# Scores of three head pairs in fp32 on the two row halves, without scales and splits, and a new order of all instructions

## The chip, the core and the metric

The kernel runs on one core of a Trainium2 chip. The engines are PE (TensorE: matrix products), DVE (VectorE), ACT (ScalarE), POOL (GpSimd) and SP (SyncE, which here only issues DMAs). The metric is the device time of one execution in microseconds, lower being better; the time of a kernel is the median of several runs.

## The reference, cut to what matters

Four batches of eight heads with 1152 keys and values of 64 elements. Queries are averaged in twos, so there are 576 of them. Attention is followed by a two-layer network with an ELU between the layers.

```python
q_pool = q.reshape(B, H, S // 2, 2, D).mean(axis=3)      # 4, 8, 576, 64
scores = np.matmul(q_pool, k.transpose(0, 1, 3, 2)) / np.sqrt(D)
scores = scores - np.max(scores, axis=-1, keepdims=True)
attn = np.exp(scores)
attn = attn / (np.sum(attn, axis=-1, keepdims=True) + 1e-09)
out = np.matmul(attn, v)                                 # 4, 8, 576, 64
x = out.transpose(0, 2, 1, 3).reshape(2304, 512)
h = x @ w_in                                             # 2304, 2048
g = np.where(h > 0, h, np.exp(np.minimum(h, 0)) - 1)
return g @ w_out                                         # 2304, 512
```

All inputs and the output are fp32.

## The kernel before

**Tiles.** The four batches are the kernel's units 0 to 3. In each, two heads go together as a pair, so a unit has four pairs. A pair has nine steps of attention: four steps of 128 pooled queries for either head, and one in which the last 64 queries of both heads share the 128 rows. That makes 36 steps in a unit and 144 in all.

**A step.** `scores` (L903, L908, L917) puts 128 x 1152 scores into the tile `s`, of which there is one. `biggest` (L932, DVE) copies the scores, scaled and with their sign turned, to a tile `ep` and takes the extreme of each row on the way. `expo` (L938, ACT) makes the exponentials and their sum. A reciprocal follows (`recip` on DVE, L946 and L947, or on POOL, L498 and L955). From there a pair goes one of two ways, by a letter in the table `SPLIT`. In a pair with "f", the probabilities are normalised in fp32 (L958 POOL, L961 DVE or L964 ACT), turned by 128 x 128 blocks on PE (L1015), copied out by ACT (L1025) or DVE (L1028) and multiplied by v in fp32 (L1047). In a pair with "s" they are split into two f16 halves (L983 POOL or L986 ACT for the high half, L989 on DVE for the low one), turned by DMA, and multiplied by split values (L1059).

**How a score is made exact in f16.** `prep` makes q and k ready for a pair. The sums of absolute values of q and k (`absum`, L558, ACT) give a power of two for each through a product with ones on PE (`summed`, L535) and four small DVE operations (L650, L492, L493, L498). With these scales q and k are split into a high f16 half (`hi`, L564 on ACT or L498 on POOL) and a low one (`lo`, L578 on DVE or L498 and L584 on POOL). In pairs 1 to 15 DMAs then turn q and k (L660, L711) and copy q's halves (L705, L708). In pair 0 (`dup`) PE turns them instead: `turned` issues 36 f16 products with a halved identity (L681), and ACT copies the results out (L684). A score is then six products: three of high with high and low together (512, 512 and 128 columns, L903), one of 128 columns (L908), and two of 512 columns that use only 64 rows of the array each and lie side by side on its two row halves (L917).

**Weights.** Both layers' weights arrive in 64-bit words. DVE decodes each piece of 512 words with three instructions (L789, L790, L793), 32 pieces in all. They are scaled and split like q and k (L816, L819, and L825 on POOL). All of that falls into unit 0. The first layer's products are L1158 and the second's L1240. Both wait for a batch's attention, so unit 0's attention has none of them to run beside it until its end.

**What sets the order.** The table `ORDER` lists every task by number with a letter for its engine: p is PE, v DVE, a ACT, g POOL, s the DMA queue of SP. The program is emitted in just that order, and each engine works through its own list strictly in turn. The table `SLOTS` names the buffer of each tile. A score task whose shape of PE's array would differ from that of the task before it issues L917 first (`turned`).

Of the kernel before, what the change touches and what calls it, by code (L numbers as in the profile page):

```python
# [32 lines left out]
0s 3s 1v 317s 2a 5a 6p 10g 337s 312s 393s 311s 7v 319v 21a 8a 22v 31p 23p 9v 11p 12a 32a 29p 25p  # L33
339v 36s 30a 27p 17p 314v 28a 395v 24a 306s 322s 438p 19p 33s 439v 13p 26a 14a 440a 441g 18a 313v
451p 38a 321s 332s 452v 308v 442a 453a 454g 15p 462p 34v 35a 39p 20a 336s 455a 463v 464a 16a 465g
324v 40v 41a 427p 447p 456p 460p 445p 46g 342s 428v 42v 4s 466a 486p 446a 43s 461a 471p 334v 429a
315a 49s 487v 458p 488a 469p 523p 457v 430g 431g 467p 472a 459v 489g 524v 468a 470a 448a 432p 436p
434p 44s 307s 437a 433v 525a 490a 475p 476v 477a 435a 47g 48s 526v 527v 510p 511v 443p 532p 338v
530p 533a 528p 531a 529a 512a 45s 50g 499p 473p 444a 449p 500v 547p 323v 51a 344v 340a 548v 513g
514a 491p 501a 52s 309v 478v 316s 325a 450a 474a 584p 492a 585v 502g 54a 479g 327s 392s 549a 503a  # L40
55p 519p 495p 496a 534p 586a 318v 536p 493p 494a 482p 483a 56v 517p 587g 537v 57a 508p 58v 509v
571p 572v 588a 518a 506p 331s 538a 62g 63g 535v 341s 539v 550v 37s 65s 310a 520a 573a 507a 504p
505v 326s 560p 561v 589p 480p 595p 484p 593p 591p 64s 540g 481a 333v 551a 59s 320a 592a 343v 485a
497p 68s 543p 590a 594a 345a 596v 328v 335a 498a 552p 553a 545p 515p 516a 556p 608p 394v 546a 562a
# [12 lines left out]
715p 790v 91v 747a 722p 767a 749a 402s 768g 726p 727v 692v 723v 378s 367s 776p 756g 777v 725a 95a
# [176 lines left out]
"""  # L234
SPLIT = ("ffff", "ssss", "ssfs", "ssss")


class Port(float):
# [99 lines left out]
def attention_moe_kernel(  # L338
# [208 lines left out]
    def prep(pr, t0, t1):  # L547
# [116 lines left out]
        def turned(name, what, key, after, bufs, to):  # L664
# [21 lines left out]
            def first_out_dve():  # L686
                nc.vector.tensor_copy(dst(), src())
# [626 lines left out]
```

## Time and profile before

| | us |
|---|---|
| median of 3 runs | 761.78 (761.12 to 762.26) |
| the profiled execution's own time | 760.01 |
| its span | 758.2 |
| PE busy | 708.5 (93%) |
| DVE busy | 628.1 (83%) |
| ACT busy | 593.5 (78%) |
| POOL busy | 372.2 (49%) |

The span is the profiled execution from its first to its last instruction; the 1.8 us around it belong to that execution's time. The profile was taken once, the median is of other runs. A busy share is an average over stages that differ: unit 0 with its weights first, then three units of attention beside the products of the batch before, and last the products of unit 3.

### The profile page before, as it was taken

The page shows a single profiled execution, that of the slowest core. Times are in us where ns is not written, and L with a number is a line of the kernel's source. Part 1 is how long each engine was busy: PE and PEld are TensorE (multiplying, and loading weights), DVE is VectorE, ACT ScalarE, POOL GpSimd, SP SyncE. Part 2 cuts the span into 40 slices and gives each one's busy share as a digit, 9 for nine tenths or more (in the row PEclk, how much of TensorE's full clock was granted, in tenths as well). Part 3 has the DMA queues.
Part 4 walks back from the last instruction along what each step waited for, and adds up shares of the span by engine and source line. Part 5 has one row for each costly group of instructions (what it writes and reads, how often), then busy time and mean ns, then how long its engine had stood idle before and what let it go on. Part 6 is the DMA issues. An engine that isn't in the chain of part 4 may idle for free. (4 is left out here: it accounts for less than half of the span.)

```text
span 758.2 us, 19529 instructions
## 1 busy us (share of the span) xinstructions
PE 708.5 (93%) x7795; PEld 468.7 (62%) x7795; DVE 628.1 (83%) x1108; ACT 593.5 (78%) x997; POOL 372.2 (49%) x396
## 2 busy tenths in 40 slices
PE   2678899999999999999999999899999999999997
PEld 1356576777555755775566566677566655775753
DVE  5999999999999988878888888989988978775331
ACT  4899899999999967797598768899888755773542
POOL 0253856659435556586424653567636345421231
PEclk9999999999999999999999999999999999999999
DMA  8688774629799999999999997899999999764001
GB/s 270 205 264 209 167 257 143 182 67 186 161 194 201 193 190 199 161 193 188 208 203 214 179 214 145 157 195 205 180 187 191 170 189 165 122 113 95 24 1 35
DMA packets 315818, 129.38 MB, mean 171 GB/s; under 512 B 290064, under 2 KB 292112, under 8 KB 315728
## 3 DMA queue, kind: packets, MB, share of 16 engines
q1 hardware_dynamic: 315728, 128.15, 84.4%
q8 instruction: 61, 1.00, 0.6%
q14 instruction: 29, 0.24, 0.1%
HBM read 45.09 MB, written 4.72 MB: 66 GB/s over the span
## 5 line engine op out<-in xcount | busy, mean ns | idle before, releaser
L932 DVE TENSOR_SCALAR_CACHE_REDUCE ep<-s,sm 128x1152 f32<-128x1152 f32 x138 | 194.8, 1412 | 23.9 <-PE s L917 12.0
L938 ACT ACTIVATE ep<-ep,wk 128x1152 f32<-128x1152 f32 x138 | 173.0, 1254 | 41.0 <-DVE ep L932 38.0
L1158 PE MATMUL r<-x,wi 128*128 128x256 f16 (+1 forms) x1536 | 197.4, 286 | 1.4 <-DVE x L1136 1.4
L1240 PE MATMUL r<-wo,g 128*128 128x512 f16 (+1 forms) x864 | 175.3, 379 | 0.6 <-POOL g L1212 0.6
L1158 PEld LDWEIGHTS <-wi 128*128 128x128 f16 x1536 | 147.8, 98 | 45.0 <-issue 6.9
L989 DVE SCALAR_TENSOR_TENSOR ep<-ep,wk,hb 128x1152 f16<-128x1152 f32 x99 | 145.7, 1479 | 12.1 <-POOL hb L983 7.1
L1240 PEld LDWEIGHTS <-g 128*128 128x128 f16 (+1 forms) x864 | 74.2, 100 | 83.3 <-issue 3.8
L903 PE MATMUL s<-kT,qT 128*128 128x512 f16 (+3 forms) x480 | 96.7, 333 | 16.8 <-DVE ep L932 11.8
L986 ACT ACTIVATE hb<-ep,wk 128x1152 f16<-128x1152 f32 x59 | 73.7, 1249 | 23.3 <-POOL wk L955 13.3
L1059 PEld LDWEIGHTS <-v 128*64 128x64 f16 x2970 | 77.9, 110 | 11.8 <-issue 11.0
L1059 PE MATMUL r<-pT,v 128*64 128x128 f16 (+1 forms) x2970 | 84.4, 215 | 0.7 <-DMA pT<-ep 0.7
L498 POOL TENSOR_SCALAR wk<-wk 128x1 f32<-128x1 f32 x61 | 23.9, 391 | 121.5 <-ACT ep L938 117.9
L903 PEld LDWEIGHTS <-qT 128*128 128x128 f16 (+1 forms) x480 | 39.2, 101 | 59.6 <-issue 34.1
L1212 POOL TENSOR_TENSOR g<-tmp,g 128x320 f16<-128x320 f32 (+1 forms) x57 | 59.0, 1040 | 33.9 <-ACT g L1208 32.7
L983 POOL TENSOR_SCALAR hb<-ep,wk 128x1152 f16<-128x1152 f32 x40 | 57.9, 1448 | 34.1 <-DMA pT<-hb 10.1
L1194 DVE SCALAR_TENSOR_TENSOR tmp<-r,tmp 128x320 f32<-128x320 f32 (+1 forms) x96 | 52.2, 550 | 21.9 <-POOL tmp L1179 12.9
L1171 ACT ACTIVATE tmp<-r 128x320 f32<-128x320 f32 (+1 forms) x96 | 45.4, 476 | 23.4 <-PE r L1158 22.3
L917 PE MATMUL s<-kT,qT 64*128 64x512 f16 (+1 forms) x320 | 57.4, 394 | 3.5 <-DVE ep L932 2.9
L1174 ACT ACTIVATE tmp<-tmp,us 128x320 f32<-128x320 f32 (+1 forms) x96 | 58.1, 611 | 1.8
L1015 PE MATMUL r<-ident,ep 128*128 128x128 f32 x351 | 50.8, 284 | 4.4 <-DVE tmp L1194 1.2
L1179 POOL TENSOR_SCALAR tmp<-tmp,us 128x320 f32<-128x320 f32 (+1 forms) x32 | 24.3, 761 | 56.7 <-ACT tmp L1174 56.3
L1216 POOL TENSOR_SCALAR g<-tmp 128x320 f16<-128x320 f32 (+1 forms) x41 | 27.1, 662 | 47.2 <-DVE tmp L1194 40.7
(149 smaller groups left out, 1047.1 us busy)
## 6 DMA issues: line engine op xcount, KB each, us to landing
k<-in_k_dram SPq DMA_DIRECT2D x16, 576.0 KB, 4.6
v<-in_v_dram SPq DMA_DIRECT2D x16, 576.0 KB, 5.0
q<-in_q_dram SPq DMA_DIRECT2D x16, 512.0 KB, 4.6
g<-in_moe_w_out_dram SPq DMA_DIRECT2D x16, 512.0 KB, 4.6
g<-in_moe_w_in_dram SPq DMA_DIRECT2D x13, 512.0 KB, 5.6
qT<-qT SPq DMA_DIRECT2D x45, 144.0 KB, 2.8
out_dram<-tmp SPq DMA_DIRECT2D x16, 256.0 KB, 3.1
pT<-ep SPq DMA_TRANSPOSE x99, 3.7
```

Source lines behind the costliest of these rows:

```text
L903: nc.tensor.matmul(s.ap[rows, c, 0:n], pr.qT.ap[:, 0, j, rows], keys[h][c], start=first[c], stop=not first[c] and c < 2, skip_group_check= ...
L917: nc.tensor.matmul(s.ap[rows, c, 0:512], pr.qT.ap[r, 1, j, rows], keys[h][c][r], start=first[c], stop=not first[c], skip_group_check=True,)
L932: nc.vector.tensor_scalar(e_(), s.ap.rearrange("p a b -> p (a b)")[:, 0:S], pr.sm.ap[:, 12:13], None, op0=ALU.mult, op1=ALU.min, accum_out ...
L938: nc.scalar.activation(out=e_(), in_=e_(), func=AF.Exp, bias=nm.ap[:, 0:1], scale=-1.0, accum_out=nm.ap[:, 1:2],)
L983: nc.gpsimd.tensor_scalar(hb.ap, e_(), nm.ap[:, 1:2], 1.0, op0=ALU.mult, op1=ALU.mult)
L986: nc.scalar.activation(out=hb.ap, in_=e_(), func=AF.Copy, scale=nm.ap[:, 1:2])
L989: nc.vector.scalar_tensor_tensor(out=e16(), in0=e_(), scalar=nm.ap[:, 1:2], in1=hb.ap, op0=ALU.mult, op1=ALU.subtract)
L1059: nc.tensor.matmul(half(h), pr.v16.ap[:, h, order[c], e], p, start=(j + c == 0), stop=(j == 2 and c == NCH - 1), skip_group_check=True,)
L1158: nc.tensor.matmul(hp.ap[:, f * n:(f + 1) * n], w_in16[g][:, a, c, (f0 + f) * 128:(f0 + f + 1) * 128], x16.ap[:, e, c, g0:g0 + n], start=( ...
L1174: nc.scalar.activation(out=en.ap[:, :m], in_=en.ap[:, :m], func=AF.Exp, scale=us.ap[:, 8:9])
L1212: nc.gpsimd.tensor_tensor(out=l, in0=gv, in1=h, op=ALU.subtract)
L1240: nc.tensor.matmul(op.ap[r0:r0 + tn, :], gt[qd].ap[:, a, fi, o:o + tn], w_out16(f // 2)[:, e, f % 2, :], start=(i < 128 // tn), stop=(i >= ...
```

## The change

For pairs 0, 1 and 2 of unit 0 (letter "F") there are no sums, scales and splits of q and k. `flip` turns k and the pooled q in fp32 on PE: k by eight 128 x 128 transposes and one block of two 64-row products, q by nine blocks of two products each, which leave the turned q twice, on the upper and the lower 64 rows. ACT or DVE copies them out to the same tiles kT and qT. A score is then two fp32 products of 512 columns, one for each half of the array's rows (the even and the odd 128-key blocks), and one of 128 columns on one half (`plain_rows`). The maximum takes a constant in place of the scale. The order of the keys in the product with v follows. The special case of pair 0 (`dup`, `turned`) is gone. An extra wait of some first-layer products for the decoded second-layer weights (`late`) is gone too. Both tables are new, so the order and the engine of tasks differ all through the program.

```diff
 ORDER = """
-0s 3s 1v 317s 2a 5a 6p 10g 337s 312s 393s 311s 7v 319v 21a 8a 22v 31p 23p 9v 11p 12a 32a 29p 25p
...
-SPLIT = ("ffff", "ssss", "ssfs", "ssss")
+SPLIT = ("FFFf", "ssss", "ssfs", "ssss")
...
-            pr.split = SPLIT[u.i][p] == "s"
+            pr.split, pr.plain = SPLIT[u.i][p] == "s", SPLIT[u.i][p] == "F"
...
+        if pr.plain:
+
+            def flip(blocks, dst, key, after, to, src):
+                xp = plan.buf("r")
+                m = 128 * len(blocks)
+
+                def flip_turn():
+                    for i, block in enumerate(blocks):
+                        for x, rows in block:
+                            to = xp.ap[rows, 128 * i:128 * i + 128]
+                            if rows == whole:
+                                nc.tensor.transpose(to, x(), ident)
+                            else:
+                                nc.tensor.matmul(to, x(), ident, start=True, stop=True, skip_group_check=True)
+
+                def flip_out():
+                    nc.scalar.activation(out=dst(), in_=xp.ap[:, 0:m], func=AF.Copy)
+
+                def flip_out_dve():
+                    nc.vector.tensor_copy(dst(), xp.ap[:, 0:m])
...
+            for h in range(2):
+                blocks = [[(lambda h=h, c=c: k32.ap[:, h, c:c + 2].rearrange("p c d -> p (c d)"), whole)] for c in range(0, 8, 2)]
+                tk_.append(flip(blocks, lambda h=h: pr.k_f()[:, 512 * h:512 * h + 512], key[9], [tk], kT, k32))
+            tk_.append(flip([[(lambda: k32.ap[:, 0, 8], upper), (lambda: k32.ap[:, 1, 8], lower)]], lambda: pr.k_f()[:, 1024:1152], key[9], [tk], kT, k32))
...
+            for a in range(0, nq, 4):
+                blocks = [[(lambda x=x: q32.ap[:, x, 0], rows) for rows in (upper, lower)] for x in range(a, min(a + 4, nq))]
+                tq_.append(flip(blocks, lambda a=a, e=a + len(blocks): pr.q_f()[:, 128 * a:128 * e], key[8], [qa], qT, q32))
...
-        if dup:
-            qflat = lambda: twice().rearrange("p e n r d -> p (e n r d)")
-            kflat = lambda: kn.ap.rearrange("p f x d -> p (f x d)")
-            pr.qs = [turned("q", [qflat, t, nq], key[8] + t, [ql, idw], [qn, qT], qT) for t in range(u.nt + 1)]
...
+            def plain_rows():
+                qf, kf = pr.q_f()[:, 128 * j:128 * j + 128], pr.k_f()
+                for r in range(2):
+                    for h, rows in jobs:
+                        p = slice(64 * r, 64 * r + 64)
+                        nc.tensor.matmul(
+                            s.ap[rows, r, 0:512], qf[p, rows], kf[p, 512 * h:512 * h + 512],
+                            start=True, stop=True, skip_group_check=True,
+                        )
+                for h, rows in jobs:
+                    p = slice(64 * h, 64 * h + 64)
+                    nc.tensor.matmul(
+                        s.ap[rows, 2, 0:128], qf[p, rows], kf[p, 1024:1152], start=True, stop=True, skip_group_check=True,
+                    )
...
-                e_(), s.ap.rearrange("p a b -> p (a b)")[:, 0:S], pr.sm.ap[:, 12:13], None,
+                e_(), s.ap.rearrange("p a b -> p (a b)")[:, 0:S], -0.5 / float(D) ** 0.5 if pr.plain else pr.sm.ap[:, 12:13], None,
...
-                    late = wo_dec if u.i == 0 and (gi > 0 or g // 2 >= 3) else []
-                    t1_ = plan.add("PE", per * 12 * mm(n), at, m1_all, [xready] + w_done[0][g] + late, [hp, x16, G], lag=45.0)
+                    t1_ = plan.add("PE", per * 12 * mm(n), at, m1_all, [xready] + w_done[0][g], [hp, x16, G], lag=45.0)
```

What stands on PE in the opening, up to the first score. Before, behind the product with ones (L535), these rows stand, each one of a run that turns k (`kn`) or q (`ep`) and with its weight load left out:

```order
L535 MATMUL r_93<-sm_89,wk 128x2
...
L681 MATMUL r_117<-hb_95,kn_91 128x128
...
L681 MATMUL r_128<-hb_95,ep_88 128x128
...
L681 MATMUL r_136<-hb_95,kn_91 128x128
...
L681 MATMUL r_158<-hb_95,ep_88 128x128
...
L903 MATMUL s_178<-kT_118,qT_129 128x512
```

The same place in the changed program; L598 is the transpose in `flip`, L600 its 64-row product, L888 and L894 the score:

```order
L598 MATMUL r_81<-ident,k_79 128x128 x4
L600 MATMUL r_93<-ident,k_79 64x128 x2
L600 MATMUL r_108<-ident,q_86 64x128 x8
L600 MATMUL r_117<-ident,q_86 64x128 x2
L600 MATMUL r_129<-ident,q_86 64x128 x8
L888 MATMUL s_138<-kT_90,qT_123 128x512 x2
L894 MATMUL s_138<-kT_90,qT_123 128x128
L598 MATMUL r_142<-ident,k_79 128x128 x4
L888 MATMUL s_160<-kT_90,qT_123 128x512 x2
```

The product with ones is gone. 24 fp32 products stand ahead of the first score, with all of q's among them; before, 26 f16 ones did.

What stands on DVE at the same time. Before, from the pooling of q (L620) to the first maximum (L932), `h` and `g` being weights and `tmp` their half-decoded form:

```order
L620 TENSOR_TENSOR q_79<-q_79 128x9x64
L650 TENSOR_SCALAR sm_89<-r_93 128x2
...
L789 TENSOR_SCALAR tmp_109<-h_86 128x512
...
L578 SCALAR_TENSOR_TENSOR kn_91<-k_83,sm_89,kn_91 128x9x64 x2
L578 SCALAR_TENSOR_TENSOR ep_88<-q_79,sm_89,ep_88 128x9x64 x2
L789 TENSOR_SCALAR tmp_146<-g_97 128x512
...
L789 TENSOR_SCALAR tmp_163<-g_99 128x512
...
L789 TENSOR_SCALAR tmp_168<-g_101 128x512
...
L932 TENSOR_SCALAR ep_192,wk<-s_178,sm_89 128x1152
```

The changed program, up to its first maximum (L938); L606 copies turned keys, L577 pools q, L776 begins a decoding:

```order
L606 COPY kT_90<-r_81 128x512
L577 TENSOR_TENSOR q_86<-q_86 128x9x64
L776 TENSOR_SCALAR tmp_104<-h_96 128x512
...
L776 TENSOR_SCALAR tmp_125<-g_98 128x512
...
L776 TENSOR_SCALAR tmp_152<-g_100 128x512
...
L938 TENSOR_SCALAR ep_158,wk<-s_138 128x1152
```

Four scale operations, four splits and one of four decodings no longer stand ahead of the first maximum; a copy of keys is new there. On SP the first load is now k's and the second q's, the other way round than before.

## Rows read from the trace of the kernel before

**Rows 1.** Busy time in stages; stage, length, then busy PE, PEld, DVE, ACT, POOL.

```profile
0.00:20.00 20.00, 5.66 (x38) 3.81 (x39) 10.53 (x22) 8.57 (x13) 0.99 (x7) 1.00 0.83 275
20.00:40.00 20.00, 13.86 (x78) 8.27 (x76) 19.31 (x35) 17.61 (x31) 7.02 (x13) 1.00 0.70 206
40.00:200.00 160.00, 141.66 (x1584) 107.29 (x1583) 155.09 (x312) 152.21 (x273) 95.05 (x73) 1.00 0.71 183
...
220.00:650.00 430.00, 424.54 (x4941) 272.60 (x4940) 374.17 (x619) 341.43 (x560) 230.95 (x255) 1.00 1.04 186
650.00:758.00 108.00, 103.96 (x964) 65.95 (x961) 49.18 (x86) 54.67 (x94) 27.24 (x41) 1.00 0.32 63
```

**Rows 2.** Timeline of the opening: start us, length us, engine, line, operation, tiles.

```profile
0.72 0.45 SPq L599 DMA_DIRECT2D q<-in_q_dram  x1
...
2.48 0.59 SPq L611 DMA_DIRECT2D k<-in_k_dram  x1
...
5.85 0.76 DVE L620 TENSOR_TENSOR q<-q 128x576 f32<-128x576 f32 x1 [4.97 <-DMA q<-in_q_dram]
...
8.51 1.16 ACT L558 ACTIVATE kn<-k 128x1152 f16<-128x1152 f32 x1 [0.63 <-DMA k<-in_k_dram]
...
17.82 1.12 PE L903 MATMUL s<-kT,qT 128*128 128x512 f16 x3 [0.26 <-ACT kT L684]
...
20.68 1.41 DVE L932 TENSOR_SCALAR_CACHE_REDUCE ep<-s,sm 128x1152 f32<-128x1152 f32 x1
```

**Rows 3.** Timeline, PE, the second score.

```profile
22.16 1.12 PE L903 MATMUL s<-kT,qT 128*128 128x512 f16 x3 [1.82 <-DVE ep L932]
...
23.85 0.61 PE L681 MATMUL r<-hb,ep 128*128 128x128 f16 x4
```

**Rows 4.** Timeline, PE, the fifth score and the turns around it.

```profile
30.93 2.82 PE L1015 MATMUL r<-ident,ep 128*128 128x128 f32 x12
33.54 0.99 PE L903 MATMUL s<-kT,qT 128*128 128x512 f16 x3
...
34.84 1.20 PE L1015 MATMUL r<-ident,ep 128*128 128x128 f32 x9
```

**Rows 5.** Timeline, PE, a score near 100 us.

```profile
100.35 0.65 PE L903 MATMUL s<-kT,qT 128*128 128x512 f16 x3
...
100.98 0.39 PE L917 MATMUL s<-kT,qT 64*128 64x512 f16 x2
101.31 0.55 PE L1015 MATMUL r<-ident,wo 128*128 128x128 f32 x3
```

**Rows 6.** Timeline, PE, an fp32 product of keys and values.

```profile
67.76 2.19 PE L1047 MATMUL r<-pT,v 128*64 128x128 f32 x36
69.88 0.55 PE L1015 MATMUL r<-ident,wo 128*128 128x128 f32 x3
```

**Rows 7.** DVE by form to 207 us: count, busy us, mean ns, idle before.

```profile
L932 DVE TENSOR_SCALAR_CACHE_REDUCE ep<-s,sm 128x1152 f32<-128x1152 f32 x39 | 55.0, 1410 | 1.7 <-PE s L917 1.2
...
L819 DVE SCALAR_TENSOR_TENSOR wi<-wi,wk,wi 128x1024 f16<-128x1024 f32 x4 | 6.3, 1567 | 0.0
L578 DVE SCALAR_TENSOR_TENSOR qn<-q,sm,qn 128x576 f16<-128x576 f32 x6 | 5.5, 921 | 0.0
...
L578 DVE SCALAR_TENSOR_TENSOR kn<-k,sm,kn 128x576 f16<-128x576 f32 x4 | 3.1, 814 | 0.0
```

**Rows 8.** ACT by form to 207 us.

```profile
L558 ACT ACTIVATE kn<-k 128x1152 f16<-128x1152 f32 x7 | 8.2, 1174 | 0.6 <-DMA k<-in_k_dram 0.6
...
L564 ACT ACTIVATE qn<-q,sm 128x576 f16<-128x576 f32 x6 | 4.7, 785 | 0.8 <-DVE sm L493 0.8
...
L684 ACT ACTIVATE qT<-r 128x512 f16<-128x512 f32 x4 | 2.4, 588 | 4.4 <-PE r L681 4.4
```

**Rows 9.** POOL by form to 207 us.

```profile
L584 POOL TENSOR_TENSOR kn<-k,kn 128x1152 f16<-128x1152 f32 x4 | 9.9, 2475 | 0.3
```

**Rows 10.** Timeline, DVE, the 46th maximum.

```profile
207.80 1.40 DVE L932 TENSOR_SCALAR_CACHE_REDUCE ep<-s,sm 128x1152 f32<-128x1152 f32 x1
```

More of the change, by code (lines that the diff above doesn't have):

```diff
@@ new lines, in load, with load_kv, qadd, q_sum @@
+        def load(src, dst):
+            def load_kv():
+                nc.sync.dma_start(
+                    out=dst.ap, in_=src[b, 2 * p:2 * p + 2].rearrange("h (p c) d -> p h c d", p=128)
+                )
+            load_kv.__name__ += "k" if src is k else "v"
+            return load_kv
+        def qadd(eng):
+            def q_sum():
+                qs = q32.ap[:, :nq, 0]
+                eng.tensor_tensor(out=qs, in0=qs, in1=q32.ap[:, :nq, 1], op=ALU.add)
+            return q_sum
@@ new lines, in prep @@
+        n = nq * 64
+        q_s = lambda: q32.ap[:, :nq, 0]
+        tq = plan.add("DMA", Move(1700.0, 2200.0), lk - 10.0, load_q, (), [q32], lag=LAND)
+        qa = plan.add("DVE", dve(n), key[0], qadd(nc.vector), [tq], [q32], [("POOL", pol2(n) + 90.0, qadd(nc.gpsimd))])
+        tk = plan.add("DMA", Move(500.0, 2200.0), lk, load(k, k32), (), [k32], lag=LAND)
+        tv = plan.add("DMA", Move(500.0, 2400.0), lk + CFG["LV"], load(v, v32), (), [v32], lag=LAND)
+        if pr.plain:
[14 more added lines that the diff above has]
+                    nc.vector.tensor_copy(dst(), xp.ap[:, 0:m])
+                mode = "col" if len(blocks[0]) == 2 else "full"
+                t = plan.add("PE", (110.0 if mode == "full" else 225.0) * len(blocks), key, flip_turn, after, [xp, src], modes=(mode, mode))
+                return plan.add("ACT", actp(m), key, flip_out, [t], [xp, to], [("DVE", dvp(m), flip_out_dve)])
+            pr.q_f = lambda: qT.ap.rearrange("p e n s -> p (e n s)").bitcast(F32)
+            pr.k_f = lambda: kT.ap.rearrange("p h c s -> p (h c s)").bitcast(F32)
+            tk_ = []
+            whole, upper, lower = slice(0, 128), slice(0, 64), slice(64, 128)
+            for h in range(2):
+                blocks = [[(lambda h=h, c=c: k32.ap[:, h, c:c + 2].rearrange("p c d -> p (c d)"), whole)] for c in range(0, 8, 2)]
+                tk_.append(flip(blocks, lambda h=h: pr.k_f()[:, 512 * h:512 * h + 512], key[9], [tk], kT, k32))
+            tk_.append(flip([[(lambda: k32.ap[:, 0, 8], upper), (lambda: k32.ap[:, 1, 8], lower)]], lambda: pr.k_f()[:, 1024:1152], key[9], [tk], kT, k32))
+            pr.kdone = [[tk_[0], tk_[2]], [tk_[1], tk_[2]]]
+            tq_ = []
+            for a in range(0, nq, 4):
+                blocks = [[(lambda x=x: q32.ap[:, x, 0], rows) for rows in (upper, lower)] for x in range(a, min(a + 4, nq))]
+                tq_.append(flip(blocks, lambda a=a, e=a + len(blocks): pr.q_f()[:, 128 * a:128 * e], key[8], [qa], qT, q32))
+            pr.qs = lambda st: tq_[2 if st.h is None else st.h]
+            pr.vdone, pr.sc, pr.sm = [tv], [], None
+            return
@@ L556, in absum @@
+        qn, kn, sm = (plan.buf(x) for x in ("qn", "kn", "sm"))
+        pr.sm = sm
         def absum(dst, src, j):
@@ L1044, in pv @@
                 for h in range(2):
[L1045 removed]
+                    o = 0 if pr.plain else h
+                    order = [*range(o, 8, 2), *range(1 - o, 8, 2), 8]
                     p = pT.ap[:, h, c] if st.h is not None else pT.ap[:, 0, c, 64 * h:64 * h + 64]
```

435 lines of the change are left out of this document (188 added, 247 removed), and 82 rows, old and new, of the table SLOTS.

## The prediction

> **What bounds the kernel now.** Four views were read in this order: busy time by stages, the timeline of the opening, PE's own timeline, and the groups by form up to 207 us. The stages [rows 1] show two kernels in one. From 220 to 650 us PE is busy for 424.5 of 430 us (98.7%), while DVE and ACT have slack: this part is as long as its products. From 40 to 200 us, where unit 0's attention and the weights are done, DVE is busy for 155.1 of 160 us (97%), ACT for 152.2 (95%) and PE for 141.7 (89%), so the two elementwise engines lead and PE has 18.3 us of gaps. Up to 20 us DVE has 10.5 us of work only.
>
> So the change has to be worked out at a point where the first part ends. I take the 46th score. There the order of either program has issued the same 204 products of the first layer, 24 of the second, 360 fp32 and 108 split products with v, and 324 turns. All later products are the same, and PE is full from there. The time is then the moment of the 46th maximum (207.80 us before [rows 10]) plus a rest that changes only by its order.
>
> **The opening.** Before, q was issued first, at 0.72 us, and DVE pooled it at 5.85; k was issued at 2.48 and used at 8.51 [rows 2]. Now k goes first and so should be there at about 5.3 (a load issued at 0.72 needs some 5 us, and k is an eighth larger). q follows at 1.3 us, and as k took 6.0 us in second place, I put q at 7.3 and its pooling's end at 8.1. PE turns k meanwhile. Of q it has nine blocks in 18 products ahead of the first score. At the low clock these cost about 0.43 us a block (four passes of 128 columns; below), 3.9 us in all, so the score starts near 12.0 and ends near 14.1. DVE has three decodings to do before the maximum, 3 x 1.8 us from about 9, when the first weights are there (before, they had been there at the latest when DVE came to them, behind four scale operations). It comes to the maximum at 14.4 us. The first maximum was at 20.68 [rows 2], which makes a lead of 6.3 us. But one decoding, 1.8 us, has only been moved behind it. The true saving of the opening is about 4.5 us: four splits at 0.8 us [rows 7] and the small operations go, less a copy; and DVE's wait shrinks by 1.6 us.
>
> **DVE and ACT up to the 46th maximum.** I counted both orders. On DVE nine splits of 576 columns go (12 to 3; six at 0.81 and three at 0.92 us [rows 7], 7.6 us). With four copies, six reciprocals and the scale chain of three pairs some 5 us more go. Three weight splits come from POOL (3 x 1.57 us, 4.7 [rows 7]), and two poolings of q, two normalisations and three small copies (4 us) come too. The sum is about -4 us; with the 1.6 us of shorter wait, DVE would be 5.5 us earlier at its 46th maximum. On ACT six sums (three of 1.17 us [rows 8], three of some 0.7) and eight splits (0.8 to 1.26 us, most at 0.79 [rows 8]) go, about 13 us. Eleven copies of 512 columns at 0.59 us [rows 8] and six small ones come where ten were, and six other copies and splits: +5 to +8. That is -5 to -8 us. Two keys' splits leave POOL (5 us each, of which 2.48 is the last operation [rows 9]); POOL was half idle, so nothing follows from it. On SP two pairs' DMA turns and copies go; PE did not wait for them there. Both leading engines thus say -5.5 us, if PE keeps up.
>
> **PE.** A score took 0.96 us near 100 us (100.35 to 101.31 [rows 5]) and 1.69 in the opening (22.16 to 23.85 [rows 3]). PE's clock is at its low level (1.2 GHz) in the first and at its high one (2.4 GHz) in the second stretch, though the stage view reads 1.00 in both; the fifth score, at 33.54, is the first that is quicker, behind twelve turns in a run [rows 4]. No fp32 score exists yet. Its nearest rows are the fp32 product with v and L917. The first issues 36 instructions of 128 columns (two to each product) in 2.12 us [rows 6]: 18 pairs lie on the two column halves, 0.118 us a pair, 0.92 ns a column and instruction. L917 shows f16 row halves side by side: two of 512 columns take 0.33 us until the next thing runs [rows 5]. If fp32 row halves also lie side by side, a score is 2 x 512 columns (0.87 to 0.94 us), 2 x 128 (0.22) and a change of shape of 0.1 us: about 1.24, or 0.28 more than before. For 27 steps that is +7.5 us. From below: if these went at half the passes, as the turns do (nine in 1.20 us [rows 4], the clock then being high), it would be 0.3 us less than before, -9 us. From above: if the halves ran one after the other, 0.87 us more a step, +31 us in all. I take the middle, since both nearest rows show overlap, and keep the ends. The turns cost eight at 0.11, one at 0.22 and nine of q at 0.22 us, 3.1 us for each of three pairs; 36 f16 products (4 us) go.
>
> Behind the sixth score PE thus has some 12 us more to do, in a stretch where it had 18 us of gaps. A score waits for the one tile `s` until DVE has read it, and DVE did not wait for scores (1.7 us before 39 maxima [rows 7]). The new order puts a decoding of 1.8 us between most early maxima, which covers a score of 1.24. I cost the tighter fit at 1.5 us. If none of it were covered it would be up to 7.
>
> **Behind the 46th score.** Counting neighbours on PE whose shapes differ, the order has 239 changes there and had 225. One shows as 0.11 us (0.33 us until the next operation, against 0.216 that 512 columns take at the high clock [rows 5]): +1.5 us. TensorEngine Tiling in the Trainium skill (Key Properties) says that a change of mode, not of tile, drains the engine. The rows agree with a gap of that kind, and by that rule more changes speak against the new order.
>
> **Sum.** -5.5 + 1.5 + 1.5 = -2.5 us against the profiled execution's own time of 760.0 us: 757.5. That execution is 1.8 us under the median 761.8, so I give the median: 759.3 us. Its own range by the two costs of PE (0 to 4 us for the first, 1 to 2 for the second) is 756 to 762.
>
> **Rivals.**
> 1. *The low clock outlasts the opening; no change.* For it: PE has waits between its early scores, and before the change the clock rose only near 34 us. Then a score costs some 2.2 us and a block of q 0.43 until the sixth. DVE's period is 1.4 + 1.8 us; where four of pair 1's blocks and a turn stand between two scores, PE needs 2.2 + 1.7 + 0.6 us. That makes DVE wait twice, 3 us in all, and the sum is +0.5: 762.3. Against it: 7 us of unbroken products from 8 us on. Of this, the Trainium skill says (TensorE: Matmul & The Clock Gate, Part 4: PE-mode transpose) that transposes do not count as busy for the clock. The rise behind a run that was mostly turns [rows 4] speaks against it here.
> 2. *PE becomes the bound of the first part; slower.* The place is the stretch from the sixth to the 46th score; it decides once scores and turns take more than the 18 us of gaps less what order and waits always leave open, about 8 us (5% of 160). 12 us against 10 is already near. If PE cannot get above 94%, some 3 to 5 us more are lost than I charged, and the sum is +2 to +3; at the upper bound of a score (halves in turn) it is some +15 to +20: 764 to 780. For it: the margin is thin. Against: the early maxima are well covered.
> 3. *A larger gain.* ACT's -8 decides, the clock rises in the opening, and the fit costs nothing: 753 to 755.
>
> **Chances.** Forecast 0.43, rival 1 0.24, rival 2 0.26, rival 3 0.07. A change under 0.2% (1.5 us) can't be told from none here. Faster is the forecast and rival 3, 0.50; same is rival 1, 0.24; slower is rival 2, 0.26. Cases of both signs hold much of it, so the range for 8 in 10 runs from rival 3's near end to the middle of rival 2: 753 to 766.
>
> **What would show it.** The first maximum near 14.4 us; fp32 scores of about 1.24 us with their row halves side by side; the 46th maximum near 204 us; PE at about 96% from 40 to 200 us and 98 to 99% from 220 to 650. If the 46th maximum is as early as that and the end is not, the rest's order is to blame. If DVE waits for scores before its maxima, rival 2 holds. If the row halves run in turn, the forecast is wrong in its largest term.

## The result, and the profile after

| | before | after |
|---|---|---|
| median, us | 762.02 (761.12 to 762.92, 4 runs) | 751.22 (749.68 to 752.42, 4 runs) |
| profiled execution's own time, us | 760.01 | 749.68 |
| span, us | 758.2 | 747.8 |
| PE, DVE, ACT busy, us | 708.5, 628.1, 593.5 | 722.1, 623.8, 583.6 |

The change makes the kernel faster: ratio 0.9857, 95% interval 0.9834 to 0.988, or 10.8 us. A second set of runs of the same kernel gave 0.9864 (0.9846 to 0.9882). The forecast was 759.3 us with a range from 753, so its sign was right and its size was not: on the profile's scale -10.3 us stand against -2.5. Every kernel below has one profile (after has two), while the times of one kernel's executions on one chip lie up to 5.5 us apart; a ratio is therefore the better measure of a run's worth.

The stages after, to set against [rows 1] (columns as there):

```profile
0.00:20.00 20.00, 11.32 (x78) 8.06 (x80) 12.94 (x23) 7.93 (x12) 1.44 (x8) 1.00 0.86 290
20.00:40.00 20.00, 18.34 (x156) 12.14 (x153) 19.29 (x38) 18.37 (x35) 5.13 (x9) 1.00 0.75 271
40.00:200.00 160.00, 153.51 (x1675) 115.74 (x1674) 153.87 (x298) 151.12 (x272) 92.83 (x86) 1.00 0.64 164
220.00:650.00 430.00, 426.08 (x5022) 275.70 (x5022) 376.84 (x620) 344.47 (x558) 220.00 (x255) 1.00 1.02 187
650.00:747.00 97.00, 93.99 (x832) 57.57 (x829) 41.30 (x75) 44.96 (x81) 30.13 (x40) 1.00 0.32 53
```

From 40 to 200 us all three engines are now at 94 to 96%, where PE stood at 89%. The part behind it is as full as it was (99%).

The opening after, to set against [rows 2]:

```profile
0.72 0.45 SPq L568 DMA_DIRECT2D k<-in_k_dram  x1
...
4.95 1.08 PE L598 MATMUL r<-ident,k 128*128 128x128 f32 x4 [4.95 <-DMA k<-in_k_dram]
...
6.94 0.76 DVE L577 TENSOR_TENSOR q<-q 128x576 f32<-128x576 f32 x1 [0.18 <-DMA q<-in_q_dram]
7.75 4.11 PE L600 MATMUL r<-ident,q 128*64 128x128 f32 x36 [1.10 <-DVE q L577]
...
11.79 1.45 PE L888 MATMUL s<-kT,qT 64*128 64x512 f32 x4
...
13.50 1.36 DVE L938 TENSOR_SCALAR_CACHE_REDUCE ep<-s 128x1152 f32<-128x1152 f32 x1
...
15.22 1.13 PE L888 MATMUL s<-kT,qT 64*128 64x512 f32 x4 [1.18 <-DVE tmp L776]
```

The first maximum comes at 13.50 us instead of 20.68. The first fp32 score begins at PE's low clock and ends at the high one (four instructions in 1.45 us; at the low level they take 2.08, as rows below show), and the second runs at the high one (1.13 us).

One fp32 score later, PE's timeline. It answers to [rows 5].

```profile
104.62 1.13 PE L888 MATMUL s<-kT,qT 64*128 64x512 f32 x4
105.59 0.38 PE L894 MATMUL s<-kT,qT 64*128 64x128 f32 x2
105.90 2.19 PE L1056 MATMUL r<-x,v 128*64 128x128 f32 x36
```

A score takes 1.28 us (104.62 to 105.90), against 0.96 in f16.

Now the cut that the prediction made, at the 46th maximum: it is at 207.80 us before [rows 10], at 201.10 after and at 203.44 in the second profile of after. The stages up to it and from it to the last product, first of before, then of after, then of the second profile of after:

```profile
0.00:207.80 207.80, 168.38 (x1765) 123.19 (x1767) 192.66 (x382) 185.21 (x326) 108.75 (x96) 1.00 0.72 191
207.80:754.30 546.50, 540.08 (x6036) 345.53 (x6031) 435.45 (x728) 407.58 (x671) 263.40 (x301) 1.00 0.91 164
```

```profile
0.00:201.10 201.10, 183.77 (x1906) 136.24 (x1907) 187.19 (x358) 178.52 (x318) 99.49 (x103) 1.00 0.68 187
201.10:744.00 542.90, 538.38 (x5994) 343.05 (x5993) 436.62 (x721) 404.35 (x662) 257.59 (x301) 1.00 0.90 164
```

```profile
0.00:203.40 203.40, 185.57 (x1906) 137.07 (x1907) 187.42 (x357) 178.44 (x318) 99.54 (x103) 0.99 0.66 185
203.40:745.30 541.90, 538.30 (x5994) 343.12 (x5993) 437.91 (x721) 404.17 (x662) 256.97 (x301) 1.00 0.90 164
```

The first part is 6.7 us shorter (4.4 in the second profile); -4.0 was forecast. The rest is 3.6 us shorter (4.6), and +1.5 was forecast. The rest has 42 products fewer (5994 for 6036) and PE 1.7 us less to do in it (540.08 to 538.38). Cut at the start of the 46th score instead, there is no such difference. First before, then after:

```profile
205.90:754.70 548.80, 541.98 (x6073) 346.87 (x6072) 437.35 (x729) 409.82 (x675) 264.26 (x302) 1.00 0.91 163
```

```profile
196.20:744.40 548.20, 542.78 (x6072) 346.27 (x6071) 441.48 (x725) 408.04 (x668) 261.13 (x303) 1.00 0.90 163
```

From the score on, both programs have the same products left (6073 and 6072 in the trace) and take the same time within 0.6 us (1.6 us to the second profile of after, by the last product). The score itself comes 9.8 us earlier (205.93 to 196.16; 7.4 us in the second profile, at 198.51). What differs is what PE does between this score and the next. PE's timeline from the 46th score to the 47th, before (the 47th is the row at 209.26):

```profile
205.93 0.68 PE L903 MATMUL s<-kT,qT 128*64 128x512 f16 x6
...
206.94 1.70 PE L1059 MATMUL r<-pT,v 128*64 128x128 f16 x54
209.26 0.39 PE L917 MATMUL s<-kT,qT 64*128 64x512 f16 x2 [0.63 <-DVE ep L932]
```

The same after (the 47th at 203.21), and below it DVE's row of the 46th maximum:

```profile
196.16 0.68 PE L909 MATMUL s<-kT,qT 128*64 128x512 f16 x6 [0.41 <-DVE ep L938]
...
197.17 1.70 PE L1068 MATMUL r<-pT,v 128*64 128x128 f16 x54
198.80 1.80 PE L1167 MATMUL r<-x,wi 128*128 128x320 f16 x12
201.58 1.79 PE L1167 MATMUL r<-x,wi 128*128 128x320 f16 x12 [0.98 <-ACT x L1077]
203.21 0.65 PE L909 MATMUL s<-kT,qT 128*128 128x512 f16 x3
```

```profile
201.10 1.41 DVE L938 TENSOR_SCALAR_CACHE_REDUCE ep<-s,sm 128x1152 f32<-128x1152 f32 x1
```

The maximum follows its score by 1.9 us before and by 4.9 after. Between the 46th score and the 47th the new order issues 24 products of the first layer, which before stand behind the 47th: twelve ahead of the maximum (1.80 us) and twelve beside it (1.79 us). So at 201.10 us PE is further along its list than it was at 207.80: it has done twelve of these products more, and all 54 products with v, of which some 30 were left before.

### The profile page after: what moved, and what is told of

The parts are those of the page before. It is cut to its first block, busy times and chain, and to the rows that moved or that the text cites. A ratio compares the mean times of both kernels' runs of the same rounds, so it can differ in the third digit from the quotient of the medians.

```text
span 747.8 us, 19687 instructions
## 1 busy us (share of the span) xinstructions
PE 722.1 (97%) x7900; PEld 479.3 (64%) x7900; DVE 623.8 (83%) x1077; ACT 583.6 (78%) x980; POOL 357.1 (48%) x404
## 4 chain that ended last, share of the span: by engine, by line
PE 52%; DVE 5%; POOL 2%; issue 1%; ACT 1%; DMA 1%; SPq 0%; POOLq 0%; ACTq 0%; DVEq 0%
PE r L1248 17%; PE r L1167 17%; PE r L1068 7%; PE s L909 5%; PE s L923 3%; DVE ep L997 2%; PE r L1023 1%; PE r L1056 1%; DVE ep L938 1%; DMA pT<-ep 1%; PE s L914 1%; ACT ep L944 0%; DVE tmp L1203 0%; POOL hb L991 0%; DMA pT<-hb 0%
## 5 line engine op out<-in xcount | busy, mean ns | idle before, releaser
L938 DVE TENSOR_SCALAR_CACHE_REDUCE ep<-s,sm 128x1152 f32<-128x1152 f32 x117 | 165.1, 1411 | 20.6 <-PE s L923 10.7
L991 POOL TENSOR_SCALAR hb<-ep,wk 128x1152 f16<-128x1152 f32 x47 | 64.5, 1373 | 63.8 <-DVE wk L953 35.1
L497 POOL TENSOR_SCALAR wk<-wk 128x1 f32<-128x1 f32 x72 | 28.6, 398 | 132.7 <-ACT ep L944 129.1
L994 ACT ACTIVATE hb<-ep,wk 128x1152 f16<-128x1152 f32 x52 | 64.7, 1250 | 26.8 <-POOL wk L961 7.9
L909 PE MATMUL s<-kT,qT 128*128 128x512 f16 (+3 forms) x390 | 76.7, 327 | 3.1 <-DVE ep L938 3.1
L1221 POOL TENSOR_TENSOR g<-tmp,g 128x320 f16<-128x320 f32 (+1 forms) x61 | 67.5, 1114 | 20.3 <-ACT g L1217 19.2
L1203 DVE SCALAR_TENSOR_TENSOR tmp<-r,tmp 128x320 f32<-128x320 f32 (+1 forms) x96 | 52.3, 552 | 28.5 <-ACT tmp L1193 13.9
L909 PEld LDWEIGHTS <-qT 128*128 128x128 f16 (+1 forms) x390 | 31.7, 100 | 33.8 <-issue 9.9
L961 POOL TENSOR_TENSOR wk<-wk 128x1 f32<-128x1 f32 x72 | 46.0, 639 | 6.0
L923 PE MATMUL s<-kT,qT 64*128 64x512 f16 (+1 forms) x260 | 45.9, 389 | 0.7 <-DVE ep L938 0.7
```

The lines of the kernel that those rows point to most:

```text
L909: nc.tensor.matmul(s.ap[rows, c, 0:n], pr.qT.ap[:, 0, j, rows], keys[h][c], start=first[c], stop=not first[c] and c < 2, skip_group_check= ...
L923: nc.tensor.matmul(s.ap[rows, c, 0:512], pr.qT.ap[r, 1, j, rows], keys[h][c][r], start=first[c], stop=not first[c], skip_group_check=True,)
L938: nc.vector.tensor_scalar(e_(), s.ap.rearrange("p a b -> p (a b)")[:, 0:S], -0.5 / float(D) ** 0.5 if pr.plain else pr.sm.ap[:, 12:13], No ...
L991: nc.gpsimd.tensor_scalar(hb.ap, e_(), nm.ap[:, 1:2], 1.0, op0=ALU.mult, op1=ALU.mult)
L994: nc.scalar.activation(out=hb.ap, in_=e_(), func=AF.Copy, scale=nm.ap[:, 1:2])
L1221: nc.gpsimd.tensor_tensor(out=l, in0=gv, in1=h, op=ALU.subtract)
```

## Experiments

Times of the 46th maximum and of the rest (from it to the end of the last product) are read from each run's profile; a ratio is to the kernel before on the same chip.

| run | ratio (95%) | 6th max., us | 46th max., us | rest, us |
|---|---|---|---|---|
| before | 1 | 38.4 | 207.8 | 546.5 |
| after | 0.9857 (0.9834 to 0.988) | 30.1 | 201.1 | 542.9 |
| after, again | 0.9864 (0.9846 to 0.9882) | 32.6 | 203.4 | 541.8 |
| 1a new operations, old order | 1.0045 (1.0028 to 1.0062) | 36.7 | 211.7 | 544.8 |
| 1b the same, placed later | 1.0058 (1.0039 to 1.0077) | 37.4 | 214.4 | 544.7 |
| 1c as 1b, k loaded first | 1.0050 (1.0033 to 1.0067) | 37.6 | 214.7 | 544.9 |
| 1d pair 0 alone | 0.9981 (0.997 to 0.9993) | 34.5 | 205.1 | 546.2 |
| 1e pairs 1 and 2 alone | 1.0136 (1.0116 to 1.0156) | 43.4 | 217.9 | 546.8 |
| 2a before, 44 products first | 1.0097 (1.0071 to 1.0123) | 41.2 | 214.5 | 545.1 |
| 2b after, a score thrice | 0.9925 (0.99 to 0.9951) | 32.2 | 203.1 | 543.6 |
| 3a after, more on PE | 0.9991 (0.9977 to 1.0006) | 32.1 | 210.9 | 542.3 |
| 3b after, more on DVE | 0.9962 (0.9947 to 0.9977) | 33.4 | 210.2 | 541.9 |
| 3c after, more on ACT | 1.0025 (1.001 to 1.0041) | 33.2 | 213.5 | 544.0 |
| 3d after, late 46th maximum | 0.9902 (0.9886 to 0.9919) | 31.4 | 207.8 | 542.0 |
| 3e before, late 46th maximum | 1.0047 (1.003 to 1.0064) | 37.9 | 212.3 | 547.6 |
| 4a after, warmed | 0.9897 (0.9879 to 0.9916) | 32.9 | 205.3 | 543.4 |
| 4b after, first score earlier | 0.9953 (0.9936 to 0.9969) | 37.7 | 208.6 | 542.5 |
| 4c after, both | 0.9901 (0.9877 to 0.9924) | 32.8 | 203.6 | 542.7 |
| 5 after, 24 products moved | 0.9903 (0.9885 to 0.992) | 34.0 | 204.8 | 545.3 |

Theories at the start: A, the gain is work taken from DVE, ACT and the opening; B, the new tables carry it; C, the clock's earlier rise does. S and W, later P, L and F, are named in the expectations.

**1. The new operations in the old order.** Every task that both programs have keeps the place, the engine and the buffer that it had before; flips and copies stand where the sums, splits and DMA turns were. Shown is where pair 1's stand (20 to 31), in 1a and, below it, in 1b.

```diff
-SPLIT = ("ffff", "ssss", "ssfs", "ssss")
+SPLIT = ("FFFf", "ssss", "ssfs", "ssss")
...
+447a 448g 307v 20p 22p 24p 26p 21a 25v 410p 430p 23a 439p 443p 27a 428p 28p 29a 325s 411v 30p 31v 3s 449a
...
+449a 469p 429a 26p 28p 444a 27a 29a 454p 317v 412a 30p 31a
...
+458p 20p 22p 24p 459v 21a 460a 23a 418a 25a 509v 510v
```

1a: 

> The new operations of all three pairs put into the order of the kernel before: loads, maxima, turns, decodings and all later work keep their old places, and the flips and their copies stand where the sums, splits and DMA turns stood. Theory A (the gain is the work that left DVE, ACT and the opening; the new tables add little): 5 to 10 us faster than before, most of it there at the 46th maximum. Theory B (the new tables carry most of the gain): -3 to +3 us. Theory C (the earlier rise of the clock carries it): as A if the clock rises before 20 us, as B if not.

1b: 

> As the first run of the new operations in the order of before, but the flips and copies of pairs 1 and 2 stand later, where their data has long been there and a PSUM tile is free, and all copies are on ACT. In the first placing the maxima lost 5 us between the third and the 13th, as PE stood waiting at pair 1's flips; that should go. Theory A (less work on DVE and ACT is the gain, in any order): 5 to 9 us faster than before. Theory B (the new tables carry most of it): -1 to -3 us, about pair 0's own part.

1c begins its order with `2s 0s` instead of `0s 2s`: 

> The same with k loaded ahead of q, as in the changed kernel: the flips of k run while q is under way. Theory S (a lead at the first maximum is kept to the end): the first maximum 1 to 3 us earlier than in the run with q first and the time shorter by as much. Theory W (the work counts): the same time as with q first.

1d has `SPLIT` "Ffff": 

> The new operations for pair 0 alone, in the order of before. A first maximum near 15 us (was 20.7) in either case. Theory S (the lead of the opening, 5 to 7 us, is kept to the end): -5 to -7 us. Theory W (DVE's and ACT's work counts, not the start): pair 0 takes four splits (3.3 us) and the small operations from DVE, so -2 to -4 us.

1e has "fFFf", placed as in 1a: 

> The new operations for pairs 1 and 2 alone, in the order of before; the opening stays (first maximum at 20.7 us). Theory S: 0 to -1 us. Theory W: -4 to -6 us, as two pairs' splits and sums leave DVE and ACT. If PE's added work (about 4 us a pair) costs time there: slower than before.

In the old order the new operations make the kernel slower, by 0.45% and 0.58%. Theory A falls, and so does the remark in the expectation of 1b that the second placing would mend the first. Theory C falls in the form that 1a's expectation gave it: PE's first two scores there, the first at 15.84 us, took 1.13 us each, so the clock had risen before 20 us, and the kernel was slower all the same (the third score took 2.08 us again). In 1c the first maximum came 1.1 us earlier than in 1b (15.71 for 16.83 us) and the ratio is the same, against theory S. Pair 0 alone (1d) gains 1.4 us, less than S or W gave it; pairs 1 and 2 alone (1e) cost 10 us, the expectation's third case. How the work went and the time did not, up to the 19th maximum (86.6 us before, 74.9 after, 91.4 in 1b), in this order of kernels:

```profile
0.00:86.60 86.60, 56.39 (x490) 38.57 (x492) 73.97 (x149) 71.84 (x129) 32.78 (x40) 1.00 0.78 227
```

```profile
0.00:74.90 74.90, 64.56 (x578) 46.24 (x580) 65.01 (x127) 60.80 (x114) 23.18 (x37) 1.00 0.65 219
```

```profile
0.00:91.40 91.40, 70.42 (x589) 48.42 (x589) 67.03 (x131) 65.67 (x121) 21.91 (x33) 0.94 0.54 186
```

DVE's work falls by 6.9 us in 1b and by 9.0 after. But in 1b DVE's idle time grows from 12.6 to 24.4 us, while after it is 9.9. Most of the growth stands in front of the maxima, as DVE's groups of 1b up to 92 us show, in the form of [rows 7]:

```profile
L1032 DVE TENSOR_SCALAR_CACHE_REDUCE ep<-s 128x1152 f32<-128x1152 f32 x14 | 19.0, 1354 | 7.3 <-PE s L988 7.1
L1032 DVE TENSOR_SCALAR_CACHE_REDUCE wo<-s 128x1152 f32<-128x1152 f32 x5 | 6.7, 1350 | 4.5 <-PE s L988 4.5
```

DVE waits 11.8 us for 19 scores, where 39 maxima had 1.7 us of waits before [rows 7]. The low clock is not the reason for most of it: 8.2 of the 11.8 us stand behind 40 us, where every score took 1.13 us or less. In 1a, up to its 19th maximum at 89.57 us, it is 4.5 us in front of the maxima and another 6.4 us in front of DVE's own copies out of the flips. This is what rival 2 described: PE is late. It comes true with the old order; the new one avoids it.

**2. Does a shift of the opening last?** 2a, in the kernel before, at the start of the program:

```diff
+    warm, into = plan.make["pT"](1), plan.make["r"](4)
+    wsrc = warm.rearrange("p h c s -> p (h c s)").bitcast(F16)
+    nc.vector.memset(wsrc[:, 0:512], 0.5)
+    for _ in range(44):
+        nc.tensor.matmul(into[:, 0:512], wsrc[:, 0:128], wsrc[:, 0:512], start=True, stop=True)
```

> The kernel before with 44 f16 products of 512 columns ahead of PE's first work, where PE stands idle for 13 us; nothing else changed. Theory C (the early clock carries the gain): the scores of the opening take 1.0 instead of 1.69 us and the time falls by 3 to 8 us. Theories A, S and W: PE waits for DVE there, so -1 to 0 us.

2b, in the changed kernel:

```diff
             if pr.plain:
+                if st.i == 0:
+                    plain_rows()
+                    plain_rows()
                 return plain_rows()
```

> The changed kernel with its first score issued three times in a row (the same values): 2.6 to 3.2 us more on PE ahead of the first maximum, nothing else. Theory S: the end comes 2.5 to 3.5 us later. Theory W: DVE catches up, 0 to 1 us.

The 44 products took longer than PE's idle time. PE's timeline of 2a:

```profile
11.71 1.24 PE L504 MATMUL r<-pT 128*128 128x512 f16 x5
12.79 0.17 PE L540 MATMUL r<-sm,wk 128*128 128x2 bf16 x1
16.27 0.29 PE L686 MATMUL r<-hb,kn 128*128 128x128 f16 x1 [3.32 <-DVE kn L583]
...
20.82 1.12 PE L908 MATMUL s<-kT,qT 128*128 128x512 f16 x3 [0.26 <-ACT kT L689]
```

The first score came at 20.82 us, 3.0 later than in [rows 2], and at the low clock again (1.12 us), so the run says little on theory C. As a delay of 3.0 us it says more: 2.9 us at the sixth maximum, 6.7 at the 46th, and a span of 763.5 us (+5.3). The growth from 2.9 to 6.7 is not the delay alone, since the granted clock of 2a was 0.83 to 0.84 in the stretches from 40 to 50 and from 60 to 80 us, where it was 1.00 before. In 2b step 0 turned out to be the fourth in the order, so the 2.6 us stand in front of the fourth maximum. The sixth came 2.1 us later than after, the 46th 2.0, the span is 750.5 (+2.7); by the medians it is more (0.9925 against 0.9857 and 0.9864, 4.6 to 5.2 us). Nothing caught up.

**3. Which engine does the first part wait for?** 3a repeats a product in the fp32 scores, 3b and 3d put idle reductions on DVE, 3c repeats ACT's copies out of the flips.

```diff
-                for h, rows in jobs:
+                for h, rows in 3 * jobs:
...
+            if st.i % 9 in (1, 3, 5, 7):
+                nc.vector.tensor_reduce(wk[:, 46:47], ident.unsqueeze(1).to_broadcast([128, 6, 128]), axis=AX.XY, op=ALU.max)
...
-                    nc.scalar.activation(out=dst(), in_=xp.ap[:, 0:m], func=AF.Copy)
+                    for _ in range(3 if pr.i else 1):
+                        nc.scalar.activation(out=dst(), in_=xp.ap[:, 0:m], func=AF.Copy)
...
+            if st.i == 44:
+                for _ in range(4):
+                    nc.vector.tensor_reduce(wk[:, 46:47], ident.unsqueeze(1).to_broadcast([128, 6, 128]), axis=AX.XY, op=ALU.max)
```

3a: 

> The changed kernel with the product of the ninth 128 keys issued three times in each of the 27 fp32 scores (the same values): two instructions of 0.11 us a product, two products more, 27 steps: 11.8 us more on PE in the first part. If PE is what the first part is as long as: 8 to 12 us slower. If DVE and ACT lead there, as the prediction had it, and PE's gaps take it up: 0 to 4 us.

3b: 

> The changed kernel with twelve idle reductions of 0.8 to 0.9 us on DVE behind twelve of the first 27 maxima: some 10 us more on DVE in the first part. If DVE is on the path there (the prediction): 8 to 10 us slower. If PE alone is: 0 to 3 us. If each of the two waits for the other in turn (theory L, a loop without slack): 6 to 10 us here as for the added products.

3c: 

> The changed kernel with each of ACT's copies out of the flips of pairs 1 and 2 made three times (the same values): ten copies, two more of each, some 10 us more on ACT in the first part. If ACT's relief was part of the gain: 4 to 10 us slower. If ACT has slack there: 0 to 2 us.

3d: 

> The changed kernel with four idle reductions on DVE (3 to 4 us in all) right ahead of the 46th maximum. The prediction took that maximum for the end of the first part: then the end comes 3 to 4 us later. Theory P (PE's place at the 46th score sets the end, and a late maximum is absorbed): 0 to 1 us, though the 46th maximum itself is 3 to 4 us later.

3e, the same in the kernel before: 

> The same four reductions at the same place in the kernel before, where the maximum stands 1.9 us behind its score's start (in the changed kernel 4.9). By the prediction 3 to 4 us later; by theory P 0 to 2 us.

What was added on DVE, from the views of `ident` in 3b and 3d:

```profile
L946 DVE TENSOR_REDUCE wk<-ident x12: 944/947/948, 14.8 to 126.7; 128x1 f32<-128x768 f32 x12
```

```profile
L940 DVE TENSOR_REDUCE wk<-ident x4: 942/952/953, 204.0 to 207.0; 128x1 f32<-128x768 f32 x4
```

Added and found at the 46th maximum, against the first profile of after: on PE 11.8 us (two products of 0.22 in 27 steps) and +9.8; on DVE 11.4 (12 x 0.95) and +9.1; on ACT 11.6 (16 copies at 0.595 and 8 at 0.26) and +12.4. In 3b and 3c a part of that is PE's clock, which fell there and not in the first profile of after (granted 0.74 from 20 to 30 us in 3b, 0.66 from 50 to 60 us in 3c). By the ratios, against both sets of after, the additions cost 9.7 to 10.2 us on PE, 7.5 to 8.0 on DVE and 12.2 to 12.8 on ACT. So most of the work added to any engine counts, which is what theory L says: scores, maxima, exponentials and turns hand one another on, and no engine's gaps take up much of what is added. In 3d the 3.8 us of reductions came out as 3.7 us between the 43rd and the 46th maximum (+3.0 and +6.7), with an unchanged rest; in 3e the 46th maximum came 4.5 us later, with a rest of 547.6 (behind PE's wait of 4.38 us the granted clock was 0.50 from 213.8 to 217 us). Theory P falls: a late maximum is not absorbed.

**4. The opening of the changed kernel.** 4a puts products of 2a's kind on PE, ten ahead of the flips and six between k's and q's. 4b and 4c change the head of the order; its first line is that of after, then come 4b and 4c.

```diff
-2s 6p 0s 7v 1v 8p 295s 320s 300s 294s 297v 12p 14p 9a 305s 13a 322v 10p 421p 4p 16s 5a 302v 11a 15a 422v 434p
+2s 6p 0s 7v 1v 8p 295s 320s 300s 294s 297v 12p 9a 305s 13a 421p 4p 10p 14p 322v 16s 5a 11a 15a 422v 302v 434p
...
+2s 6p 0s 7v 1v 8p 295s 320s 300s 294s 297v 12p 9a 305s 13a 421p 4p 10p 14p 16s 5a 11a 15a 422v 322v 302v 434p
```

After, again: 

> The changed kernel once more, beside the three runs that vary its opening: 0.985 to 0.987 of the time before.

4a: 

> The changed kernel with ten f16 products of 512 columns on PE ahead of the first flips and six between those of k and of q, so that the clock is up for the flips of q (18 pairs at 0.11 instead of 0.22 us); the place of DVE's work is unchanged, three decodings stand before the first maximum. The first maximum is DVE's (13.5 us), so by theory S, which counts the first maximum alone, no change: within 1 us of the changed kernel. Theory C (the clock of the opening itself is worth time): 2 to 3 us faster.

4b: 

> The changed kernel with the first score straight behind the one copy of q that it needs, and one decoding of 1.8 us moved from ahead of the first maximum to behind it; no other clock. First maximum near 12.3 us (13.5). Theory S: 1.2 us faster than the changed kernel. Theory W (the work ahead of the 46th maximum counts, and it is the same): no change.

4c: 

> Both edits, and a second decoding moved behind the first maximum: the first maximum near 10.6 us. Theory S: 2.5 to 3 us faster than the changed kernel, which would make it the fastest of all. Theory W: no change.

None of the three beats the changed kernel, so no version found here does. In 4c the first maximum came at 10.87 us, 2.6 earlier, and the sixth 2.6 later than in the first profile of after. So theory S is wrong as written: a lead at the first maximum alone is worth nothing. Rows of DVE and PE in 4b show what took it there:

```profile
12.66 1.36 DVE L933 TENSOR_SCALAR_CACHE_REDUCE ep<-s 128x1152 f32<-128x1152 f32 x1 [1.30 <-PE s L889]
...
23.81 0.43 DVE L771 TENSOR_SCALAR tmp<-g 128x512 uint32<-128x512 uint32 x1 [2.75 <-DMA g<-in_moe_w_in_dram]
27.27 2.08 PE L883 MATMUL s<-kT,qT 64*128 64x512 f32 x4 [4.36 <-DVE ep L933]
...
34.66 1.36 DVE L933 TENSOR_SCALAR_CACHE_REDUCE wo<-s 128x1152 f32<-128x1152 f32 x1 [1.69 <-PE s L889]
```

The decodings between the early maxima wait for weights; PE waits meanwhile, its clock falls, and then DVE waits for slow scores. This differs from one execution to the next, as four profiles show whose programs are the same up to there. The wait for weights in front of the fourth maximum is 0.25 us in the first profile of after, 1.27 in 3d, 1.19 in the second profile of after and 1.12 in 5; the sixth maximum of these three comes 1.3, 2.5 and 3.9 us later than in the first profile. In 3d the clock stayed high. In the other two the fourth score ran at the low one; rows of the second profile of after:

```profile
23.40 2.08 PE L888 MATMUL s<-kT,qT 64*128 64x512 f32 x4 [2.20 <-DVE ep L938]
...
25.93 1.36 DVE L938 TENSOR_SCALAR_CACHE_REDUCE ep<-s 128x1152 f32<-128x1152 f32 x1 [0.80 <-PE s L894]
```

DVE's waits for slow scores in front of the fourth and fifth maxima are 1.25 us there (0.80 and 0.45) and 2.78 in 5 (0.80 and 1.98). From there on a shift lasts. In 4a to 4c, 2b, 5 and the second profile the sixth maximum lies 2.1 to 7.6 us behind that of after, and the 46th behind its own by the same within 0.2 us, 4a's excepted (+2.8, then +4.2).

**5. The 24 products.** In the order of the changed kernel:

```diff
-1941p 1948p 400a 936p
+400a 936p 1941p 1948p
```

> The changed kernel with the 24 first-layer products that stand on PE between the 46th score and the 47th moved behind the 47th. From the 46th maximum to the last product it takes 542.9 us (before: 546.5). Theory F (the rest is shorter because the order fills the wait for that maximum with products that stand behind it in the kernel before): PE waits about 4 us there, the products (3.4 us) come later, the rest grows to 545 to 546.5 and the time by 2.5 to 3.5 us. If the rest is shorter for another reason: 0 to 1 us.

PE's timeline of this run, from behind the 46th score:

```profile
200.88 1.70 PE L1063 MATMUL r<-pT,v 128*64 128x128 f16 x54
206.27 0.39 PE L918 MATMUL s<-kT,qT 64*128 64x512 f16 x2 [3.70 <-DVE ep L933]
206.59 0.66 PE L904 MATMUL s<-kT,qT 128*128 128x512 f16 x3
207.09 0.22 PE L909 MATMUL s<-kT,qT 128*128 128x128 f16 x1
207.15 5.10 PE L1162 MATMUL r<-x,wi 128*128 128x320 f16 x24
```

PE waits 3.70 us, the rest grows from 542.9 and 541.8 us to 545.3, and the ratio from 0.9864 to 0.9903 (3.0 us). The numbers are those of theory F, but a part of them is PE's clock, which fell behind that wait. From the first of the 24 products to PE's next other work it is 4.9 us here (207.15 to 212.08); in after, twelve of them need 1.63 (201.58 to 203.21), so 24 need 3.3. In the stage view of this stretch the granted clock, the third number from the end, is 0.54:

```profile
207.10:210.60 3.50, 3.50 (x17) 2.01 (x16) 3.47 (x5) 2.51 (x6) 0.74 (x1) 0.54 0.71 138
```

So some 1.7 us of the growth are the low clock, and 0.7 to 1.8 us are the order as such. Theory F holds in its direction; its size is in part the clock's.

## Why the prediction was wrong

- **The opening** was right, in the first profile. The first maximum came at 13.50 us (forecast 14.4), the score in front of it at 11.79 (12.0). Nine blocks of q took 4.11 us, 0.46 each (0.43).
- **An fp32 score** was right: 1.28 us (1.24), with its row halves side by side; four instructions of 512 columns in turn would have taken 1.7, twice the 0.87 that the prediction gave two. The Trainium skill (TensorEngine Tiling (Array Packing), Key Properties) says that tiles run independently and in parallel; the row at 104.62 agrees, for fp32 too.
- **Work up to the 46th maximum** was right in size: DVE -5.5 us (192.66 to 187.19; forecast -4), ACT -6.7 (-5 to -8). DVE's idle time went from 15.1 to 13.9 us, or 16.0 in the second profile (forecast -1.6 + 1.5). In sum -6.7 and -4.4 were found, and -4.0 forecast. That this is so near is in part luck: the changed kernel is ahead by 7.2 us at the first maximum, 11.6 at the 19th, 13.4 at the 36th, 3.0 at the 41st and 6.7 at the 46th, as each order has put other work between the maxima.
- **The step that failed** is "The time is then the moment of the 46th maximum plus a rest that changes only by its order", with +1.5 us for that order. The products were counted up to the 46th score, but the time was taken at its maximum. At that maximum the two orders stand at different places of PE's list: the new one has 42 products fewer left, and the rest is 3.6 to 4.6 us shorter, not 1.5 longer. Timed at the score, where the products were counted, the first part is 9.8 us shorter and the rest 0.5 us (7.4 and 1.6 in the second profile). This stood in the order of the instructions and could have been read there. The term makes 5.1 of the 7.8 us of the miss in the first profile and 6.1 of 6.5 in the second. How much of it the 24 products ahead of the 47th score carry is shown in part: putting them back made the rest 2.4 to 3.5 us longer, some 1.7 of that by the low clock. The other runs bear out that the rest goes with the order: under the old order the rest is 544.7 to 547.6 us in eight profiles, under the new one 541.8 to 544.0 in ten, whatever was delayed ahead of it; only the fifth run, with 545.3, leaves that range, and without the low clock it would not.
- **The changes of shape on PE**, forecast at +1.5 us behind the 46th score, can have added no more than 0.8 us: that is how much the busy time for the same products grew (541.98 to 542.78).
- **PE's fit**, +1.5 us, was the right worry with the wrong cause. With the new operations in the old order DVE had to wait 11.8 us for scores in 1b, and the kernel lost 3.4 us in 1a and 4.4 in 1b; with the new order it waited 2.5 us for 45 scores (0.6, 0.8 and 1.1 us for its three forms in the same view). So the new operations alone do not bring the gain. Against the two placings tried by hand in the old order the new tables are worth 1.8 to 2.0%, 14 to 15 us; a better placing might leave less. The other cross was not run: the old operations in an order made anew for them. So it is not shown how much of the 10.8 us needs the new operations at all.
- **Rivals.** Rival 1 (low clock) fell as written: the second score already took 1.13 us, and the kernel was faster. But the clock can fall again behind it, as in the second profile of after and in 5, where DVE then waited 1.25 and 2.78 us for slow scores. Rival 2 came true only without the new order. Rival 3 named the right side, but not the cause.
- **Slips in its sums**, none of which bears on the miss: by its two costs its own range is 757 to 762, not 756 to 762; rival 2's 3 to 5 us make the sum +0.5 to +2.5, not +2 to +3; 0.3 us less in 27 steps is -8 us, not -9.
- **Left open.** How much of the 4.4 to 6.7 us of the first part is the clock's earlier rise. In 2a and 4a the clock fell again while PE waited, so no run had the old opening at the high clock throughout. 1a shows that an early rise is not enough. And it stays open where the 2.7 us come from that the first profile's 46th maximum was earlier than forecast; the second profile, with 0.4, says that most of it is the difference between two executions.

The line `late`, whose extra wait was described as gone, changed nothing: it never reached the program, as tasks are emitted by the tables alone.

## What to carry to other kernels

Count work and time at the same event of the same engine. Where two engines take turns, read from the order what stands on each of them between the event that you count to and the event that you time. In a loop where three engines hand one another on, work taken from one of them can turn into waiting, as it did here in the old order; most of the work that was added to any of them, and a delay once the loop ran, stayed to the end. Where a run makes an engine wait, look at its clock behind the wait before calling the whole difference the order's.

## What the runs showed of the hardware

In these runs PE's clock fell again behind waits. The ten leading products of 4a were followed by flips and a score at the high level, then a wait of 3.81 us, and the next score was at the low level. PE's timeline of 4a:

```profile
10.07 1.13 PE L900 MATMUL s<-kT,qT 64*128 64x512 f32 x4
...
15.82 2.08 PE L900 MATMUL s<-kT,qT 64*128 64x512 f32 x4 [3.81 <-DVE ep L950]
```

The same four instructions take 1.13 us at the one level (2.4 GHz) and 2.08 at the other (1.2 GHz). The length of the wait does not decide alone: at the fourth score the clock was low behind waits of 2.20 us (second profile of after) and 2.13 (5), and high behind 2.27 (3d, 1.13 us). It is not only a matter of the opening: near 210 us it fell behind waits of 3.70 us (5) and 4.38 (3e), and not behind 3.02 (3d).
